# One product of the first layer normalisation, on VectorE instead of GpSimd

## The chip, the cores and the metric

The kernel runs on one core of a Trainium2 chip. The time is device microseconds of one execution, the median of several runs: 138.59 us before the change (three runs, 138.46 to 138.66). Beside the times there is one profiled execution with its trace. The engines are called as the profile calls them: PE (TensorE, matmuls) with PEld (its weight loads), DVE (VectorE), ACT (ScalarE), POOL (GpSimd) and SP (SyncE, which here only issues transfers).

## What is computed

One decoding step of a transformer layer for a batch of four tokens: layer normalisation, attention over a window of a cache, and a gated feed-forward part, each added to its input.

```
def _layernorm(x, axis=-1, eps=1e-5):
    m = jnp.mean(x, axis=axis, keepdims=True)
    v = jnp.var(x, axis=axis, keepdims=True)
    return (x - m) / jnp.sqrt(v + eps)

def _A_ref(x, k_cache, v_cache, wq, wo):        # 32 heads of 128, 4 key/value heads
    W = min(4096, max(256, Sk // 4))            # 2048 of 8192 positions
    q = (x @ wq).reshape(B, Sq, Hq, Dh).transpose(0, 2, 1, 3)
    k = jnp.repeat(k_cache[:, :, Sk - W:, :], rep, axis=1)
    v = jnp.repeat(v_cache[:, :, Sk - W:, :], rep, axis=1)
    p = _softmax(jnp.einsum("bhqd,bhkd->bhqk", q, k) * (Dh ** -0.5))
    o = jnp.einsum("bhqk,bhkd->bhqd", p, v)
    return o.transpose(0, 2, 1, 3).reshape(B, Sq, Hq * Dh) @ wo

def _B_ref(x, w1, w3, w2):                      # 1024 -> 3584 -> 1024
    return (_silu(x @ w1) * (x @ w3)) @ w2

h  = x + _A_ref(_layernorm(x), ...)
h2 = h + _B_ref(_layernorm(h), ...)
```

All inputs and the output are bf16. With four tokens every weight and every cached key and value is used for very little arithmetic: 55.6 MB are read for a result of 8 KB.

## The kernel before

All large inputs pass through one buffer in SBUF, `ring`, of five units of 32 KB in each of the 128 partitions. SyncE issues their loads in one fixed order (`load`, L127): `wq` in two pieces (slice 0 of eight, then slices 1 to 7), four loads of keys, four of values, `wo`, `w1`, `w3`, and `w2` in six pieces. A load whose place in the ring is still in use waits on SyncE's queue, and with it the loads behind it: the last two loads of values take the place of `wq`, so they wait for the query projection (L249); `w1` waits for the second attention output (L397); `w3` for the output projection (L484). ScalarE issues the small load of `x` (L139) and shares the output stores with SyncE.

The order of all work is written out by hand (`manual_schedule`), one program for each engine; an instruction that needs another engine's result waits on a semaphore, and a second wait at one place takes a semaphore instruction of its own. The stages are:

1. GpSimd builds identities, masks and constants (L147 to L201).
2. `x` is transposed on VectorE (L234) and normalised (`layernorm_T`, below), which gives `n_T`: the normalised input, transposed, as 8 slices of 128 partitions by 32 columns, of which 4 columns hold the tokens and the rest is zero.
3. The query projection: 64 matmuls (L249), eight for each of the eight slices of `wq`, with `n_T` as the stationary operand. The result is copied to SBUF (L259), transposed (L262), and spread into `Qm` (L269), which GpSimd has filled with zeros (L266).
4. Keys are transposed on TensorE (L283) and copied back by VectorE and ScalarE in turn (L285, L287), scores computed (L306), softmax (L318 to L378), attention outputs (L397), GpSimd sums (L414, L415).
5. The output projection (L484), the residual, and the second normalisation by the same `layernorm_T`.
6. The gate and up projections (L510), the gating, and the down projection (L560, L608), whose second part follows the landing of the last pieces of `w2`. VectorE and ScalarE write the result (L641 to L646) and four small stores take it out.

`layernorm_T` works on 8 slices by 4 tokens, 32 columns, in each of 128 partitions. ScalarE writes the input and its squares to `both` (L206, L207); one matmul with a matrix of 1/1024 sums over the partitions (L209); VectorE adds the eight slices (L211), which gives mean and mean square; GpSimd forms the variance (L215, L216); ScalarE takes the root (L217); VectorE the reciprocal, `rstd` (L220). Meanwhile GpSimd fills `n_T` with zeros (L222) and subtracts the mean, which gives `hc` (L224). The last step is the product of `hc` and `rstd` into `n_T` (L227). Behind it on GpSimd stand the fills of `Qm` and `oP` (L266, L268). The buffers of a normalisation (`both`, `mean`, `rstd`, `hc`) are the same ones both times; `n_T` has one for each.

Of the kernel before, what the change touches and what calls it, by code (L numbers as in the profile page):

```python
# [21 lines left out]
def kernel(  # L22
# [20 lines left out]
    nc = tc.nc  # L43

    B, _, D = A_x.shape
# [11 lines left out]
    S = R // B  # L57
# [142 lines left out]
        out=gather[:, :, :B], in_=ident[:].rearrange("p (c b s) -> p c b s", c=C, b=B)[:, :, :, 0]  # L200
    )  # L201

    def layernorm_T(h_T, tag):

        both = act.tile([P, 2, KC, B], FP32, tag="ln_both")
        nc.scalar.copy(out=both[:, 0], in_=h_T)  # L206
        nc.scalar.activation(out=both[:, 1], in_=h_T, func=ACT.Square)  # L207
        sums_ps = ps.tile([P, 2, KC, B], FP32, tag="scB")
        nc.tensor.matmul(sums_ps[:], lhsT=mean_f[:], rhs=both[:], start=True, stop=True)  # L209
        mean = act.tile([P, 2, B], FP32, tag="ln_mean")  # L210
        nc.vector.tensor_reduce(  # L211
            out=mean[:], in_=sums_ps[:].rearrange("p t k b -> p t b k"), axis=AX.X, op=ALU.add
        )
        rstd = act.tile([P, 1, B], FP32, tag="ln_rstd")
        nc.gpsimd.tensor_tensor(out=rstd[:, 0], in0=mean[:, 0], in1=mean[:, 0], op=ALU.mult)  # L215
        nc.gpsimd.tensor_tensor(out=rstd[:, 0], in0=mean[:, 1], in1=rstd[:, 0], op=ALU.subtract)  # L216
        nc.scalar.activation(  # L217
            out=rstd[:, 0], in_=rstd[:, 0], func=ACT.Sqrt, bias=eps_t[:], scale=1.0
        )
        nc.vector.reciprocal(out=rstd[:, 0], in_=rstd[:, 0])  # L220
        n_T = act.tile([P, KC, R], BF16, tag=tag + "_nT")
        nc.gpsimd.memset(n_T[:], 0.0)  # L222
        hc = act.tile([P, KC, B], FP32, tag="ln_hc")
        nc.gpsimd.tensor_tensor(  # L224
            out=hc[:], in0=both[:, 0], in1=mean[:, 0:1, :].to_broadcast([P, KC, B]), op=ALU.subtract
        )
        nc.gpsimd.tensor_tensor(  # L227
            out=n_T[:, :, :B], in0=hc[:], in1=rstd[:].to_broadcast([P, KC, B]), op=ALU.mult
        )
        return n_T  # L230

    def transpose_quads(dst, src, n):

        nc.vector.transpose(  # L234
            out=dst.rearrange("p j r -> p (j r)"), in_=src.rearrange("p (q j) -> p j q", j=n)
        )

    x_T = act.tile([P, KC, R], BF16, tag="xT")
    transpose_quads(x_T[:], x_nat[:], KC)
    xn_T = layernorm_T(x_T[:, :, ::S], "ln1")  # L240


    q_ps = ps.tile([P, 2, REP // 2, Dh], FP32, tag="scA")
# [253 lines left out]
        nc.scalar.copy(out=h1[2 * R * k : 2 * R * k + 2 * R, :], in_=y_ps[:, k])  # L497
    h_T = act.tile([P, KC, R], FP32)
    transpose_quads(h_T[:], h1[:], KC)
    hn_T = layernorm_T(h_T[:, :, :B], "ln2")  # L500


    FJ = FC // 2
# [180 lines left out]
```

## Time and profile before

| what | value |
|---|---|
| median of three runs | 138.59 us |
| the profiled execution's own time | 138.48 us |
| its span, first to last instruction | 136.7 us |
| bytes read | 55.58 MB |
| mean granted clock of TensorE | 0.871 |
| transfer of `wo` lands (SyncE's wait for it) | 82.0 us |
| last wait for a transfer ends on TensorE | 132.88 us |

Times inside the trace are microseconds from the start of the span. In a line of the page such as `PE 80.7 (59%) x779` stand the busy time, its share of the span and the number of instructions. A line of a timeline has the start, the duration, engine, line, operation, the names written and read, and in brackets how long the engine had been idle before and what ended that. A line of the chain of waits has the start, the duration and what ran. A line of the table of stretches has the stretch and its length, then the busy time of PE, PEld, DVE, ACT and POOL with the number of instructions, then TensorE's granted clock, the mean busy share of the sixteen DMA engines, and GB/s. The packet records, which the trace holds behind these views, give start, duration and size of each packet that a DMA engine moved; a load ends with one packet of four bytes on each engine that took part.

### The profile page before, as it was taken

How to read it: one execution, taken by the hardware profiler on the slowest of the kernel's cores; microseconds unless marked ns; L12 is line 12 of the kernel's file. 1: busy time of each engine (PE TensorE's matmuls, PEld its weight loads, DVE VectorE, ACT ScalarE, POOL GpSimd, SP SyncE). 2: the span in 40 equal slices, each digit the busy share in tenths (PEclk: the TensorE clock that was granted, in tenths of full speed). 3: DMA queues.
4: the chain of work that ended last, by engine and by line, in shares of the span. 5: the costliest groups of instructions: out<-in, count | busy, mean ns of one | idle time of the engine just before them, and what ended most of it. 6: DMA issues, size and time to landing. Idle time of an engine off the chain costs nothing.

```text
span 136.7 us, 1804 instructions
## 1 busy us (share of the span) xinstructions
PE 80.7 (59%) x779; PEld 43.5 (32%) x779; DVE 48.6 (36%) x45; ACT 29.9 (22%) x35; POOL 17.7 (13%) x50
## 2 busy tenths in 40 slices
PE   0000044959999985129992993995198000999770
PEld 0000022449966941023332340541043000444440
DVE  0000110007625463899299922001100297062022
ACT  3000140027959495013000000002501700000100
POOL 7600061000000000000084633000300000001000
PEclk9999999999999999855698699999856855569998
DMA  4999697999999999998978979969899798999960
GB/s 168 525 420 538 269 537 307 436 417 446 417 422 441 412 432 422 417 590 360 556 326 384 537 326 475 520 285 537 352 453 508 302 520 364 397 414 423 403 235 2
DMA packets 2782, 55.69 MB, mean 407 GB/s; under 512 B 312, under 2 KB 600, under 8 KB 728
## 3 DMA queue, kind: packets, MB, share of 16 engines
q1 hardware_dynamic: 2740, 55.58, 95.3%
q8 instruction: 6, 0.10, 0.3%
q10 hardware_dynamic: 36, 0.01, 0.0%
HBM read 55.58 MB, written 0.01 MB: 407 GB/s over the span
## 4 chain that ended last, share of the span: by engine, by line
DMA 56%; PE 30%; DVE 6%; ACT 3%; SPq 1%; issue 1%; DVEq 0%
DMA ring<-in_B_w_dram 40%; DMA ring<-in_A_wq_dram 16%; PE kt_ps L283 9%; PE sc_ps L306 5%; PE o_ps L397 5%; PE gate L510 4%; PE q_ps L249 4%; DVE P L360 2%; DVE PT L382 2%; SPq L128 1%; ACT ring L287 1%; PE small L397 1%; DVE ring L285 1%; DVE rmax L318 1%; ACT q_sb L259 1%
## 5 line engine op out<-in xcount | busy, mean ns | idle before, releaser
L287 ACT COPY ring<-kt_ps 128x2048 bf16<-128x2048 bf16 x8 | 14.6, 1866 | 7.1 <-PE kt_ps L283 7.1
L283 PE MATMUL kt_ps<-ident,ring 128*128 128x128 bf16 x256 | 15.0, 219 | 0.6 <-DVE Qm L269 0.5
L283 PEld LDWEIGHTS <-ring 128*128 128x128 bf16 x256 | 14.4, 98 | 2.6 <-issue 1.7
L414 POOL TENSOR_TENSOR o<-od 128x256 f32<-128x256 f32 x4 | 6.8, 1696 | 55.5 <-DVE od L405 55.5
L285 DVE COPY ring<-kt_ps 128x2048 bf16<-128x2048 bf16 x8 | 9.8, 1225 | 9.3 <-PE kt_ps L283 9.3
L510 PE MATMUL up<-ring,n_T 128*32 128x448 bf16 x64 | 6.0, 568 | 10.9 <-DMA ring<-in_B_w_dram 10.9
L209 PE MATMUL sums_ps<-both,mean_f 128*128 128x64 f32 x4 | 1.1, 366 | 19.0 <-ACT both L207 19.0
L397 PE MATMUL o_ps<-ring,PT 128*128 128x512 bf16 x32 | 11.5, 541 | 0.0
L510 PEld LDWEIGHTS <-n_T 128*32 128x32 bf16 x128 | 5.1, 143 | 20.3 <-DMA ring<-in_B_w_dram 11.5
L397 PEld LDWEIGHTS <-PT 128*128 128x128 bf16 x64 | 7.6, 121 | 10.3 <-issue 5.7
L532 DVE RECIPROCAL eg<-eg 128x896 f32<-128x896 f32 x1 | 5.8, 5753 | 10.9 <-ACT eg L531 10.9
L360 DVE TENSOR_TENSOR P<-p,gmask 128x2048 bf16<-128x2048 bf16 x4 | 9.1, 2278 | 0.8 <-ACT p L347 0.8
L382 DVE STREAM_TRANSPOSE PT<-P 128x2048 bf16<-128x2048 bf16 x4 | 9.2, 2306 | 0.1
L249 PE MATMUL q_ps<-ring,n_T 128*32 128x512 bf16 x64 | 6.2, 556 | 3.6 <-DMA ring<-in_A_wq_dram 1.8
L306 PE MATMUL sc_ps<-ring,Qm 128*32 128x512 bf16 x64 | 7.6, 605 | 0.4 <-DVE ring L285 0.4
L510 PE MATMUL gate<-ring,n_T 128*32 128x448 bf16 x64 | 5.9, 558 | 3.0 <-DMA ring<-in_B_w_dram 3.0
L397 PE MATMUL small<-ring,PT 128*128 128x512 bf16 x32 | 7.2, 379 | 0.0
L484 PE MATMUL y_ps<-ring,oP 128*32 128x512 bf16 x64 | 7.1, 379 | 0.1
L209 PEld LDWEIGHTS sums_ps<-both,mean_f 128*128 128x128 f32 x4 | 0.8, 249 | 19.4 <-issue 17.1
L234 DVE STREAM_TRANSPOSE x_T<-x_nat 128x256 bf16<-128x256 bf16 x1 | 0.6, 626 | 15.9 <-DMA x_nat<-in_A_x_dram 15.9
L560 PE MATMUL early_ps<-ring,hg_T 128*32 128x512 bf16 x42 | 5.0, 379 | 1.1 <-DMA ring<-in_B_w_dram 1.1
L464 ACT CAST oP<-on_ps 128x128 bf16<-128x128 f32 x1 | 0.3, 266 | 22.6 <-PE on_ps L457 22.6
(94 smaller groups left out, 68.9 us busy)
## 6 DMA issues: line engine op xcount, KB each, us to landing
ring<-in_B_w_dram SPq DMA_DIRECT2D x2, 7168.0 KB
ring<-in_A_k_cache_dram SPq DMA_DIRECT2D x4, 2048.0 KB, 25.6
ring<-in_A_v_cache_dram SPq DMA_DIRECT2D x4, 2048.0 KB, 42.8
ring<-in_A_wq_dram SPq DMA_DIRECT2D x1, 7168.0 KB, 21.2
ring<-in_B_w_dram SPq DMA_DIRECT2D x1, 3328.0 KB
ring<-in_B_w_dram SPq DMA_DIRECT2D x1, 2048.0 KB, 23.3
ring<-in_A_wq_dram SPq DMA_DIRECT2D x1, 1024.0 KB, 4.5
ring<-in_B_w_dram SPq DMA_DIRECT2D x1, 1024.0 KB
```

The lines of the kernel that those rows point to most:

```text
L249: nc.tensor.matmul(q_ps[R * c : R * c + R, hf], lhsT=xn_T[:, kc, :], rhs=wq_s[:, kc, o : o + HALF * Dh], start=(kc == 0), stop=(kc == KC - 1),
L283: nc.tensor.transpose(out=kt_ps[:, jj], in_=blocks[:, jj, :], identity=ident[:])
L285: nc.vector.tensor_copy(out=blocks, in_=kt_ps[:])
L287: nc.scalar.copy(out=blocks, in_=kt_ps[:])
L306: nc.tensor.matmul(sc_ps[b // 2][R * q : R * q + R, b % 2], lhsT=Qm[:, b, g * R : (g + 1) * R], rhs=kT[:, b, g, q], start=(g == 0), stop=( ...
L360: nc.vector.tensor_tensor(out=P4[:], in0=stage.pop(("p1", b))[:].rearrange("p (x o) -> p x o", o=1).to_broadcast([P, JR * L5, Hkv]), in1=g ...
L382: nc.vector.transpose(out=PT[:].rearrange("p j h -> p (j h)"), in_=stage.pop(("P4", b))[:].rearrange("p x g -> p (x g)"),)
L397: nc.tensor.matmul(o_ps, lhsT=PT[:, i * JM : (i + 1) * JM, :].rearrange("p j h -> p (j h)"), rhs=v_s[b][:, i * JM : (i + 1) * JM, :], star ...
L414: nc.gpsimd.tensor_tensor(out=o2[:], in0=od[:, :2], in1=od[:, 2:], op=ALU.add)
L484: nc.tensor.matmul(y_ps[R * i : R * i + R], lhsT=oP[:, t, :], rhs=row[:, i], start=False, stop=(t == T - 1), tile_position=(0, R * i), ski ...
L510: nc.tensor.matmul(out_ps[hf][R * c : R * c + R, :], lhsT=hn_T[:, kc, :], rhs=cols[:, kc, c, hf], start=(kc == 0), stop=(kc == KC - 1), ti ...
L532: nc.vector.reciprocal(out=eg[:], in_=eg[:])
```

## The change

`layernorm_T` takes the engine of its last product as an argument. The first normalisation passes VectorE, the second GpSimd, as before. All other instructions keep their engines and their order.

```
-    def layernorm_T(h_T, tag):
+    def layernorm_T(h_T, tag, eng):
...
-        nc.gpsimd.tensor_tensor(
+        eng.tensor_tensor(
             out=n_T[:, :, :B], in0=hc[:], in1=rstd[:].to_broadcast([P, KC, B]), op=ALU.mult
         )
         return n_T
...
-    xn_T = layernorm_T(x_T[:, :, ::S], "ln1")
+    xn_T = layernorm_T(x_T[:, :, ::S], "ln1", nc.vector)
...
-    hn_T = layernorm_T(h_T[:, :, :B], "ln2")
+    hn_T = layernorm_T(h_T[:, :, :B], "ln2", nc.gpsimd)
```

VectorE's program has two instructions more than before: the product and a wait.

## The prediction

> **What bounds the kernel now.** I read the page first for how busy each engine is, then a table of stretches, then the chain of waits, and last the order of instructions around the first normalisation. The first question is which resource has no idle time.
>
> ```profile
> PE 80.7 (59%) x779; PEld 43.5 (32%) x779; DVE 48.6 (36%) x45; ACT 29.9 (22%) x35; POOL 17.7 (13%) x50
> DMA packets 2782, 55.69 MB, mean 407 GB/s; under 512 B 312, under 2 KB 600, under 8 KB 728
> q8 instruction: 6, 0.10, 0.3%
> HBM read 55.58 MB, written 0.01 MB: 407 GB/s over the span
> ```
>
> No compute engine is busy for more than 59% of the span, while 55.58 MB of weights and cache are read. The stretches show where the DMA engines pause (the last two columns are their busy share and the rate):
>
> ```profile
> 2.00:22.00 20.00, 1.70 (x10) 0.79 (x11) 1.03 (x3) 3.27 (x5) 6.00 (x26) 1.00 1.01 429
> 22.00:42.00 20.00, 17.82 (x259) 13.02 (x259) 6.42 (x6) 9.15 (x6) 0.00 (x0) 1.00 1.01 429
> 62.00:82.00 20.00, 17.34 (x62) 7.18 (x61) 14.84 (x11) 0.78 (x2) 7.43 (x6) 0.78 0.98 423
> 102.00:122.00 20.00, 9.05 (x104) 3.82 (x96) 8.48 (x4) 3.15 (x3) 0.00 (x0) 0.59 0.95 409
> 132.00:137.00 5.00, 1.22 (x31) 0.66 (x18) 0.71 (x2) 0.26 (x1) 0.00 (x0) 0.86 0.08 26
> ```
>
> They don't pause: from 2 us to 132 us the share is about 1 (a packet counts in the stretch where it starts, hence 0.95 and 1.01). So the time is a start of about 2 us, a stream of 130 us, and a tail. The chain of waits seems to say something else for the middle:
>
> ```profile
> 22.44 5.17 PE q_ps L249 x56
> ...
> 68.07 1.74 PE small L397 x8
> 69.81 0.02 issue
> 69.83 29.46 DMA ring<-in_B_w_dram
> ...
> 132.84 0.04 issue
> 132.88 0.36 PE y_ps L608 x6
> ```
>
> From 22.44 to 69.81 us it runs through TensorE, since the w1 load (L448) is issued only once L397 has freed its ring space. But the DMA engines still had the wo load to move then: SyncE's next load waits 12.2 us more for wo, until about 82.0. The w1 load moves 7168 KB (7.34 MB), which at 429 GB/s takes 17.1 us; it ends at 99.28, and 82.0 + 17.1 = 99.1. So it flowed right behind wo, and its issue had some 12 us to spare. TensorE's early work is on the printed chain, yet it doesn't set the end.
>
> Now the place of the change:
>
> ```profile
> 18.79 0.24 POOL L224 TENSOR_TENSOR hc<-both,mean 128x32 f32<-128x32 f32 x1
> 18.95 0.18 DVE L220 RECIPROCAL rstd<-rstd 128x4 f32<-128x4 f32 x1 [0.93 <-ACT rstd L217]
> 19.27 0.24 POOL L227 TENSOR_TENSOR n_T<-hc,rstd 128x32 bf16<-128x32 f32 x1 [0.25 <-DVE rstd L220]
> 19.45 0.63 POOL L266 MEMSET Qm<- 128x640 bf16 x1
> 19.57 1.04 PE L249 MATMUL q_ps<-ring,n_T 128*32 128x512 bf16 x8 [1.81 <-POOL n_T L227]
> 22.44 5.15 PE L249 MATMUL q_ps<-ring,n_T 128*32 128x512 bf16 x56 [1.83 <-DMA ring<-in_A_wq_dram]
> ```
>
> The product ends at 19.51. Eight matmuls follow, on the first slice of wq, which is there; then TensorE stands for 1.83 us until the other seven slices have landed.
>
> **The change part by part.** *Removed from GpSimd:* one product of 0.24 us and the semaphore instruction before it (17 ns). *Added to VectorE:* a wait and a product; these are its two instructions.
>
> When can the product start? The reciprocal ends at 18.95 + 0.18 = 19.13. Now the hand-over to GpSimd takes 19.27 - 19.13 = 0.14 us. A VectorE instruction that waits for VectorE's own last result is in the trace: the reciprocal of L532 ends at 108.64 + 5.75 = 114.39 and L533 starts at 114.50, 0.11 us. So the start is about 19.24. The other input, hc, ends at 19.03 and is there.
>
> How long is it? No VectorE product of 32 columns is in the trace. From below, the reciprocal of 128x4 took 178 ns; from above, the copy of 128x128 took 292 ns. Between the products of 448 (625 ns) and 896 columns (1092 ns) a column costs 467/448 = 1.04 ns, and 625 - 416 x 1.04 = 192 ns for 32; the reduction of 64 columns took 224. I take 0.21 us. The product then ends at 19.45, 0.06 us sooner than now. By the ends, it starts at 19.20 to 19.27 and lasts 0.18 to 0.29: 19.38 to 19.56, so from 0.13 sooner to 0.05 later.
>
> *TensorE's wait.* Its first weight load of L249 waits for GpSimd alone, as both the zeros of n_T (L222) and the product come from there. Afterwards they come from two engines. Where TensorE already waits for two at one place, a semaphore instruction of its own stands there (51 ns at L320; GpSimd's at L227 took 17 ns). I add one such: 0.02 us, 0.05 at most. The zeros are written by 18.83, so it holds nothing up. Queued behind it is TensorE's whole program, so its cover matters. The first eight matmuls end at about 20.57 (20.71 at worst) instead of 20.61, and the next needs wq at 22.44. The shift is swallowed by that idle time: 0.00 us. If that cover were gone, the same 0.13 sooner to 0.10 later would reach q and the scores, and the 12 us of the w1 load would swallow it there.
>
> *Queued behind, elsewhere.* On VectorE it is the copy to Qm (L269), at 29.43, ten microseconds on. On GpSimd the zeros of Qm and oP move up from 19.45 to about 19.1; L269, at 29.43, is the first to need them. In the second normalisation the product stays on GpSimd, and its buffers were last read by VectorE some 78 us before. No DMA is moved past anything.
>
> *Do the two engines hinder each other?* GpSimd's sum at L414 took about 2.7 us beside VectorE's products and 0.72 us without, so they can. Here it would stretch the zeros of Qm, say fourfold to 2.5 us: done by 22.6 with those of oP, still 6.8 us early. Were VectorE the one to stand instead, for the 0.63 us of one fill, the product would end at 20.1 and the eight matmuls at 21.2, before 22.44. Nothing in both cases.
>
> The sum: 138.48 (the profiled execution: 136.7 span and 1.8 around it) + 0.00. That execution lies 0.11 below the median of the three runs, so against the median I forecast 138.6.
>
> **The rivals.** *First, a clock that dips in the tail (slower).* TensorE's granted clock is 0.59 between 102 and 122 us and 1.00 from 122 to 132. If a half-speed stretch falls on the last landing, the six matmuls between it and VectorE's result (0.36 us) take 0.72: 138.59 + 0.36 = 138.95. It decides from the point where the half-speed stretch that now ends at 122 lasts to 133. For it: the stretches begin and end at multiples of 3.41 us from each other (57.13, 67.37, 74.20, 77.61), and the change moves TensorE's first burst by a few hundredths. Against: three runs lie within 0.2 us, and TensorE's 2.4 us of idle time between 124 and 133 soaks up a short dip. [...]
>
> *Second, an instruction block that meets a loaded DMA engine (slower).* The page lists six instruction packets; in the packet records each is 16 KB and takes 1.03 to 1.10 us, at 34.0, 40.7, 50.0, 82.4, 105.6 and 130.8 us, every one in step with TensorE's program. What they do can be read from the sixteen completions of each load: before the first they lie within 0.55 us; after it one engine is 1.3 us late, then two, three, four and five, the same lateness each, so each block hit another engine. The one 128 KB load in 16 partitions makes four more engines late by 1.8 us. They finish last, at 132.72; those that a block delayed finish just before. One instruction more in TensorE's program, or another start of it, could put a block on one of those four: the end moves by about 1.65 (late completions at 128.35 to 128.48 against the others at about 126.8), 140.2. For it: the margin between good and bad is one engine. Against: six blocks remain six, since the seventh edge would lie some 250 instructions on and TensorE has some 40 left; VectorE's program has about 70 instructions and no block of its own in the span. [...]
>
> *Third, the end of the stream evens out (faster).* The engines end their last loads between 132.1 and 132.72. If the blocks fell so that all ended at the mean, about 132.4, the tail would start 0.3 sooner: 138.3. For it: the same sensitivity. Against: the four engines with the small load stay late whatever the blocks do.
>
> *Fourth,* the change doesn't come to pass as said, for instance the product waits again behind GpSimd's fills (0.63 + 0.95 us): n_T at 21.0, the eight matmuls done by 22.1, still hidden; 138.6.
>
> **How the numbers follow.** A difference of 0.2%, 0.28 us, is about what a measurement of this kernel can tell from no change. The forecast, all hidden, gets 0.58, the fourth case 0.04: same 0.62. The clock gets 0.11, the block 0.08, and 0.05 goes to what I don't see on that side: slower 0.24. The evened end gets 0.10, and 0.04 for the unseen: faster 0.14. The range reaches below to the evened end with a tenth for the spread of the runs, 138.2, and above to the clock's 138.95 and as much as the runs' spread of 0.2 again, 139.2; it leaves out the block and part of the unseen. The likeliest case alone is 138.4 to 138.8.
>
> **What would show it.** Right: VectorE's product of 128x32 near 0.2 us, n_T's first use at 19.4 to 19.6, TensorE idle before 22.4 for 1.8 to 2.0 us, the last landing near 132.8, DMA share near 1 throughout. Wrong: wq landing at another time; seven instruction packets, or one followed by completions 3 us late; a granted clock of 0.5 around 133; or any new wait of SyncE's queue that ends after the DMA engines have run dry.

## The result, and the profile after

The changed kernel takes 139.89 us (median of five runs, 139.81 to 140.02) against 138.58 us before: a ratio of 1.0098, 95% interval 1.0083 to 1.0113. It is 1.3 us slower. The forecast was 138.6, no change, and the range ended at 139.2.

The page of the profile after, with the span, the busy times and the DMA queues:

```profile
span 137.6 us, 1802 instructions
PE 79.3 (58%) x777; PEld 42.9 (31%) x779; DVE 48.7 (35%) x46; ACT 29.9 (22%) x35; POOL 17.5 (13%) x49
DMA packets 2783, 55.70 MB, mean 405 GB/s; under 512 B 312, under 2 KB 600, under 8 KB 728
q8 instruction: 6, 0.10, 0.3%
q14 instruction: 1, 0.01, 0.0%
```

Two things are to be seen. The span grew by 0.9 us only, so some 0.5 us of the loss lies around it. And there is one packet more than before, on a queue that the page of before doesn't list: an instruction packet.

First the place of the change, in the timeline after:

```profile
19.09 0.24 POOL L224 TENSOR_TENSOR hc<-both,mean 128x32 f32<-128x32 f32 x1
19.25 0.18 DVE L220 RECIPROCAL rstd<-rstd 128x4 f32<-128x4 f32 x1 [0.93 <-ACT rstd L217]
19.27 0.63 POOL L266 MEMSET Qm<- 128x640 bf16 x1
19.53 0.19 DVE L227 TENSOR_TENSOR n_T<-hc,rstd 128x32 bf16<-128x32 f32 x1
19.77 1.04 PE L249 MATMUL q_ps<-ring,n_T 128*32 128x512 bf16 x8 [1.72 <-DVE n_T L227]
22.49 5.29 PE L249 MATMUL q_ps<-ring,n_T 128*32 128x512 bf16 x56 [1.67 <-DMA ring<-in_A_wq_dram]
```

The product takes 0.19 us on VectorE and ends 0.29 us after the reciprocal, where it was 0.38 before. (All of the stage lies 0.3 us later, since x landed 0.3 us later in this execution.) TensorE then waits 1.67 us for wq, as it did. Nothing was lost here. The stretches after show the stream as full as before, and the chain of waits ends it at nearly the same time:

```profile
2.00:22.00 20.00, 1.70 (x10) 0.78 (x11) 1.22 (x4) 3.27 (x5) 5.78 (x25) 1.00 1.00 428
102.00:122.00 20.00, 9.21 (x108) 4.07 (x100) 9.47 (x6) 3.15 (x3) 0.00 (x0) 0.66 0.95 408
132.00:137.00 5.00, 1.39 (x40) 0.84 (x29) 0.81 (x3) 0.26 (x1) 0.00 (x0) 0.90 0.08 26
```

```profile
133.04 0.04 issue
133.08 0.36 PE y_ps L608 x6
```

The loss is in the last four microseconds, behind the last landing. SyncE waits there for the output stores (engine and line, what it waited for, us in total, times, longest). Before:

```profile
SPq L679 <- DMA out_dram<-res: 1.0, 2, 0.7
```

and after:

```profile
SPq L679 <- DMA out_dram<-res: 2.0, 2, 1.8
```

Behind the stores comes the closing barrier of the program (listed under L679). An engine enters it with a drain, which here ends 0.05 us behind the engine's last computing instruction (VectorE before: 134.05 and 134.01). Its instructions on VectorE, by the view of that line (duration in ns, shortest, median and longest, then the first and last start), before:

```profile
L679 DVEq EVENT_SEMAPHORE  x2: 21/21/21, 135.8 to 136.6; - x2
L679 DVEq DRAIN  x2: 143/322/500, 133.6 to 136.3; - x2
```

and after:

```profile
L679 DVEq EVENT_SEMAPHORE  x2: 21/21/21, 137.1 to 137.6; - x2
L679 DVEq DRAIN  x2: 19/134/248, 134.0 to 137.2; - x2
```

Before, VectorE was released in the barrier at 135.80 and started its second drain at 136.32, half a microsecond later; after, it follows within 0.11 (137.09 to 137.21). Its first drain shows the reverse: before, it started at 133.55, beside the last result instruction (L646, 133.58); after, at 134.01, 0.23 us behind it. So the barrier before held a stall of 0.4 us that is gone, and yet the end is later. The records of the trace put the pieces together. For each kernel that was run: the start of VectorE's first result instruction (L642, right behind the last landing; where lines were added it has a later number), the last store's completion after that, from there to the end of the span, what the execution took outside the span, its time, and when 8 KB instruction packets moved (from the start of the span on).

```
                     L642   store   barrier  around   time    8 KB packets
                     starts done    to end   span
before              133.26   2.17    1.25     1.79   138.48   136.99 137.18
after               133.47   3.26    0.90     2.26   139.89   134.66 138.63
two fills only      133.63   3.39    1.24     1.79   140.05   135.14 138.76
length undone       133.77   2.17    1.27     2.03   139.24   137.76 137.92
GpSimd's length     133.63   3.44    1.27     1.79   140.13   135.18 138.82
one fill            133.54   2.18    1.24     1.89   138.85   135.68 137.46
both edges early    134.18   2.17    0.91     1.79   139.05   118.20 127.22
one and five        133.75   2.17    0.92     1.79   138.62   128.43 135.71
five on GpSimd      134.62   2.17    1.26     1.83   139.88   127.50 138.37
two and five        134.39   3.26    0.91     1.83   140.39   127.93 135.59
product, old length 133.61   2.18    1.27     1.79   138.85   137.35 137.54
beside the stores   133.43   2.17    0.90     1.87   138.38   135.68 136.39
```

After against before: 0.21 at L642, 1.09 at the stores, -0.35 in the barrier, 0.47 around the span; together 1.4, the difference of the two profiled executions.

The stores' part shows in the packet records after. Each of the four stores moves four packets of 512 bytes, on four DMA engines. The instruction packet runs from 134.66 to 135.25; one packet of each store starts at 135.25, 135.28, 135.31 and 135.34, right behind it, while the other twelve had ended by 135.10. Three of the four completions of the last store come at 135.61 to 135.64 and the fourth at 136.72. Before, all four came at 135.30 to 135.43.

### The profile page after: what moved, and what is told of

It is laid out like the page before. It is cut to its first block, busy times and chain, and to the rows that moved or that the text cites. A ratio compares the mean times of both kernels' runs of the same rounds, so it can differ in the third digit from the quotient of the medians.

```text
span 137.6 us, 1802 instructions
## 1 busy us (share of the span) xinstructions
PE 79.3 (58%) x777; PEld 42.9 (31%) x779; DVE 48.7 (35%) x46; ACT 29.9 (22%) x35; POOL 17.5 (13%) x49
## 4 chain that ended last, share of the span: by engine, by line
DMA 56%; PE 30%; DVE 6%; ACT 3%; SPq 1%; issue 1%; DVEq 0%
DMA ring<-in_B_w_dram 40%; DMA ring<-in_A_wq_dram 15%; PE kt_ps L283 9%; PE sc_ps L306 5%; PE o_ps L397 4%; PE gate L510 4%; PE q_ps L249 4%; DVE P L360 2%; DVE PT L382 2%; ACT ring L287 1%; SPq L128 1%; PE small L397 1%; DVE ring L285 1%; DVE rmax L318 1%; ACT q_sb L259 1%
## 5 line engine op out<-in xcount | busy, mean ns | idle before, releaser
L510 PE MATMUL up<-ring,n_T 128*32 128x448 bf16 x64 | 4.5, 452 | 10.8 <-DMA ring<-in_B_w_dram 10.8
```

Source lines behind the costliest of these rows:

```text
L510: nc.tensor.matmul(out_ps[hf][R * c : R * c + R, :], lhsT=hn_T[:, kc, :], rhs=cols[:, kc, c, hf], start=(kc == 0), stop=(kc == KC - 1), ti ...
```

## The experiments

The theory that came out of this, called the length theory below, is my reading of the packet records: each instruction packet (8 KB at 136.99 and 137.18 before, at 134.66 and 138.63 after) is taken for a block of one engine's program; VectorE's program, two instructions longer, meets a block's edge two instructions earlier, ahead of its first drain instead of ahead of its second, and the packet that goes with the edge then moves together with the stores (0.59 us from 134.66) and holds up one of their DMA engines. The rival, the product theory: it is the product on VectorE itself, or what it shifts behind the normalisation. Medians and ratios below are against the kernel before on the same chip, whose median was 138.80 for the first four, 138.61 for the next four and 138.73 for the last two.

The fills that make a program longer are all of this kind, ahead of the normalisation, where both engines have nothing to do:

```
+    pad = const.tile([1, 64], FP32)
+    for i in range(2):
+        nc.vector.memset(pad[:, i : i + 1], 0.0)
...
     def layernorm_T(h_T, tag):
```

**Two fills only.** The edit above on the kernel before; the product stays on GpSimd.

> The kernel before, product on GpSimd, with two fills of one number each put early into VectorE's program. Length theory (VectorE's program, two instructions longer, reaches the edge of an 8 KB instruction block before its last drain, and the fetch of the next block holds up one of the DMA engines that carry the output stores): an 8 KB instruction packet near 134.6 us, the last store's completion 1.1 to 1.3 us later than before, 139.4 if GpSimd's program of the old length costs nothing, up to 139.9 if it stands at its own edge in the last barrier. Product theory (what costs is the product on VectorE, in the first normalisation): 138.6, no packet at 134.6.

139.96 us, ratio 1.0083 (1.0068 to 1.0098). Nearly the whole loss, 1.16 of 1.31 us, is there without the change. The page and SyncE's waits of this kernel:

```profile
span 138.3 us, 1804 instructions
...
q14 instruction: 1, 0.01, 0.0%
...
SPq L683 <- DMA out_dram<-res: 2.2, 2, 1.9
```

The packet is there, at 135.14, and SyncE's longest wait for the stores is 1.9 us. The barrier is 1.24 long although VectorE's stall is gone from it; the time around the span is 1.79. So this kernel loses in the barrier what the changed one loses outside.

**The length undone.** The changed kernel, with a small copy that runs twice moved from VectorE to ScalarE, and two fills on GpSimd.

```
-        nc.vector.tensor_copy(out=bias[:], in_=nm_ps)
+        nc.scalar.copy(out=bias[:], in_=nm_ps)
...
+    for i in range(2):
+        nc.gpsimd.memset(pad[:, 32 + i : 33 + i], 0.0)
```

> The changed kernel, product on VectorE, but VectorE's program two instructions shorter elsewhere (the two small copies of the bias, L341, on ScalarE) and two fills added on GpSimd, so both programs have the length of before. Length theory: 138.6, no instruction packet of 8 KB before 136.9, VectorE's stall of 0.45 us back in the last barrier. Product theory: 139.9 still.

139.63 us, 1.0053 (1.0037 to 1.0068), with nine runs from 139.00 to 140.01: neither expectation. The tail of the profiled execution (139.24) is as the length theory expected: stores done after 2.17, packets at 137.76 and later, VectorE's second drain 0.5 us late. But the time is not that of before, and the copy on ScalarE changed more than the length: TensorE and ScalarE got an instruction more each, L642 starts 0.5 us later, and the runs spread over 1 us. Its tail speaks for the length theory; its time decides nothing. The ninth experiment does it more cleanly.

**GpSimd's length back.** The changed kernel with the two fills on GpSimd alone.

> The changed kernel with two fills added on GpSimd, so that only VectorE's program is longer than before. The span grew by 0.94 us and the time around it by 0.5. If the 0.5 is GpSimd's program, two instructions shorter, which meets its own block edge after the span: the time around the span is back to 1.8 us, the 8 KB packet after the span comes earlier, and the stall moves into the last barrier (span 138.0) or vanishes (span 137.6): 139.9 or 139.4. If the 0.5 has to do with VectorE alone: around the span 2.3, 139.9.

139.91 us, 1.0077 (1.0060 to 1.0094). The time around the span is back at 1.79, and the barrier is at 1.27 instead of 0.90. So the 0.47 us around the span were GpSimd's: by the length theory its program, two instructions shorter, met its own edge behind the last instruction of the span. With the old length it meets it in the barrier, where VectorE's stall had covered it before. The time is as good as that of the changed kernel, 1.1 us above the kernel before: what left the space around the span came back in the barrier.

**One fill.** The kernel before with one fill on VectorE.

> The kernel before with one fill put early into VectorE's program. Length theory: the edge lies one instruction later than in the changed kernel, behind the drain, where VectorE waits for the stores anyway; the fetch comes near 135.4, after the stores' packets: no delay of the stores, 138.1 to 138.6 (138.1 if only VectorE's stall was on the path of the last barrier, 138.6 if GpSimd stands there as long). Without the length theory one instruction more should cost half of what two cost: about 139.2.

138.82 us, 0.9999 (0.9990 to 1.0008). One instruction costs nothing, two cost 1.2 us. Of the length theory's two cases it is the one in which GpSimd stands in the barrier as long. The lines of this kernel, of SyncE's waits, the queues and the barrier:

```profile
SPq L683 <- DMA out_dram<-res: 1.0, 2, 0.7
...
q14 instruction: 1, 0.01, 0.0%
...
L683 DVEq DRAIN  x2: 24/265/506, 133.8 to 136.2; - x2
```

The packet is in the span as in the changed kernel, but at 135.68, when the stores' packets had ended (135.23): they are not late. VectorE's second drain comes at 136.21, 0.12 after its release at 136.09. Now it is GpSimd that stands: 0.38 us between its last drain's end (136.39) and its next instruction (136.77), against 0.04 after. That is why the barrier is no shorter.

**Both edges early.** The changed kernel with four fills more on VectorE and seven on GpSimd.

> The changed kernel, product on VectorE, with four fills more early in VectorE's program (six instructions more than before) and seven on GpSimd (five more than before). Length theory: VectorE meets its edge while it waits for the last matmuls and GpSimd while it waits for the stores, so the stall of some 0.45 us that one of the two showed in the last barrier of each kernel so far is gone, VectorE's packet comes near 133, ahead of the stores, and GpSimd's near 125 to 126: 0.4 us below the kernel before on the same chip, the product on VectorE notwithstanding. Product theory: 1.1 to 1.3 us above it.

139.03 us, 1.0038 (1.0023 to 1.0054), 0.4 above, which neither theory has. The product is on VectorE and about two thirds of its supposed cost (1.1 to 1.3) is absent, but the gain that the length theory forecast isn't there either. Both stalls are gone (0.91), but both packets moved in the stream of weights, at 118.2 and 127.2, VectorE's far sooner than expected, and there they cost too. Of the four completions of the small load that lands after the first packet, one comes at 125.07, 0.9 us behind the next; in the loads after the second packet another is 0.5 us late as well, and L642 starts at 134.18.

**One and five fills.** The kernel before, one fill on VectorE, five on GpSimd.

> The kernel before with one fill more on VectorE and five on GpSimd. Length theory: with one alone the stall of 0.4 us stood on GpSimd instead of VectorE; with five there too nobody stands in the last barrier, VectorE's packet comes behind the stores: 0.4 us below the kernel before. If the stall on GpSimd isn't what held the barrier: no change.

138.71 us, 1.0018 (1.0003 to 1.0033). The barrier is 0.92: with one fill alone it was GpSimd that stood there. What this saves, GpSimd's packet at 128.4 takes back in the stream: the last completion of the last load comes at 133.66, 0.38 us behind the next. In the four kernels with a packet in the stream that gap is 0.38 to 0.70 us, in the other eight at most 0.30. In size this is less sure, since L642 starts as late as here (133.75) in a kernel without such a packet too (133.77 with the length undone).

**Five fills on GpSimd alone.**

> The kernel before with five fills more on GpSimd alone. Length theory: VectorE still stands 0.45 us at its edge in the last barrier, so no change, within 0.1 us of the kernel before. If GpSimd's edge alone held the barrier: 0.4 us below.

139.46 us, 1.0062 (1.0043 to 1.0080), which neither expectation has. VectorE's stall is in the barrier as expected (1.26). The rest is ahead of the stores: GpSimd's packet at 127.50 makes the next piece of w2 late in one of its sixteen completions (129.84, the others by 129.12), and the chain of waits of this execution then runs through matmuls at a lower clock (the second line is of the table of stretches, its granted clock third from the end):

```profile
129.88 3.02 PE early_ps L564 x16
```

```profile
132.00:135.00 3.00, 2.65 (x45) 1.54 (x40) 1.18 (x4) 0.26 (x1) 0.00 (x0) 0.68 0.16 55
```

Before, the same sixteen took 1.90 us. How much of the median is the packet and how much the clock, one profile can't say.

**Two and five fills.** The kernel before, two on VectorE, five on GpSimd.

> The kernel before with two fills more on VectorE and five on GpSimd. Length theory: VectorE's packet meets the stores as in the changed kernel, which costs 1.1 us, and no stall is left in the last barrier, which saves 0.4: 0.6 to 0.8 us above the kernel before. If the delay of the stores and the stalls aren't separate sums: 1.1 to 1.3 above.

139.61 us, 1.0069 (1.0055 to 1.0084), 1.0 above; between the two expectations. GpSimd's packet moved in the stream here too (127.93, and the last completion of the last load is 0.61 us behind the next). The profiled execution, at 140.39 the slowest of the five, also shows a lower clock (0.65 between 132 and 135), so what each of the two added is not told apart. Stores and barrier add up as separate pieces: the stores 3.26 as in the changed kernel, the barrier 0.91 as with both edges away.

**The product on VectorE at the old length.** The changed kernel without the reciprocal, and one fill on GpSimd.

```
-        nc.vector.reciprocal(out=rstd[:, 0], in_=rstd[:, 0])
...
+    for i in range(1):
+        nc.gpsimd.memset(pad[:, 32 + i : 33 + i], 0.0)
```

> The changed kernel, product on VectorE, without the reciprocal in either normalisation (L220 left out, so the product is with the root itself): VectorE's program is then as long as before, and one fill brings GpSimd's to its length of before. TensorE's and ScalarE's programs are untouched. Length theory: the time of the kernel before within 0.2 us, no instruction packet before the stores are done, VectorE's stall back in the last barrier. Product theory: 1.1 to 1.3 us above.

138.81 us, 1.0000 (0.9991 to 1.0009). With the product on VectorE and the lengths of before, the time is that of before, and so is the tail: the queues list no packet of that kind in the span, SyncE's wait and VectorE's late drain are back.

```profile
q1 hardware_dynamic: 2740, 55.58, 95.2%
q8 instruction: 6, 0.10, 0.3%
q10 hardware_dynamic: 36, 0.01, 0.0%
...
SPq L682 <- DMA out_dram<-res: 1.0, 2, 0.7
...
L682 DVEq DRAIN  x2: 144/320/496, 133.9 to 136.7; - x2
```

**The edges beside the stores.** The kernel before with one fill on VectorE, three on GpSimd, and a last GpSimd instruction that waits for the first store, so that GpSimd meets its edge while the other stores run.

```
                 out=out_flat[:, c * DQ : (c + 1) * DQ], in_=res[R * c : R * c + B, :]
             )
+            if c == 0:
+                nc.gpsimd.memset(res[:B, :1], 0.0)
```

> The kernel before with one fill on VectorE, which puts VectorE's edge behind its drain, three on GpSimd, and one more on GpSimd at the end that waits for the first output store, so that GpSimd meets its edge while the last stores are under way, behind the stream and ahead of the barrier. Length theory: no block is fetched in the stream, none before the stores, and nobody stands in the last barrier: 0.4 us below the kernel before. If a block of GpSimd's still meets the stores or is asked for early, in the stream: as before or 0.3 to 1 us above, and its packet will show where.

138.47 us, 0.9977 (0.9969 to 0.9986): faster than both kernels, by 0.3 us against before. The packets are at 135.68 and 136.39, behind the stores' packets, the stores are done after 2.17, the barrier takes 0.90.

```profile
span 136.5 us, 1810 instructions
...
q14 instruction: 2, 0.02, 0.0%
...
SPq L687 <- DMA out_dram<-res: 1.0, 2, 0.7
```

## Why the prediction was wrong

*What was right.* The product takes 0.19 us (0.21 forecast), ends 0.09 sooner after the reciprocal (0.06 forecast), and is swallowed by the wait for wq (1.67 us); the fills on GpSimd move up and nobody notices; the stream stays full; TensorE's chain through the middle doesn't set the end. The ninth experiment shows the cost of the product itself: none, within 0.1%. One detail was wrong without consequence: TensorE got no semaphore instruction more (12 before and after).

*The step that failed* is in the second rival: "VectorE's program has about 70 instructions and no block of its own in the span". The mechanism of that rival, a block that meets a loaded DMA engine, is by the length theory the one that struck, but I tied it to TensorE's program and to the weights, priced it at 1.65 us there and gave it 0.08. I read "in the span" as "far from it". The records of before had two 8 KB instruction packets at 136.99 and 137.18, 0.3 and 0.5 us behind the span's end, and a drain of VectorE's that stood 0.4 us in the closing barrier: by the length theory VectorE was at an edge already, two instructions from its first drain (one fill has the packet at 135.68, two have it at 135.14), with the stores right before it. So the sum put two instructions more on VectorE at 0.00 once their run time was hidden; two empty ones alone measured 1.16 us, 1.09 of the changed kernel's loss is in the stores, and with the product on VectorE but the lengths of before nothing is lost. The prediction's own sign came, seven instruction packets in the span, on VectorE's side instead of TensorE's.

*The second failure* is the sum's "1.8 around it", taken as fixed. It held the other half of the edit: GpSimd's program became two instructions shorter, by the length theory its edge moved behind the span (a packet at 138.63), and the time around it became 2.26. Two fills put it back to 1.79. In the whole time this mattered little, since the barrier then took 1.27 instead of 0.90: 1.11 us above the kernel before with GpSimd's length back, 1.31 without.

*The other rivals.* The clock did dip in the tail, most in two profiles with a packet in the stream (0.68 and 0.65 between 132 and 135), but not in that of the changed kernel (1.00 from 122 to 135). The end of the stream didn't even out: the last completion comes at 133.36 against 133.17 before.

*The packets by size.* In the records before, the six packets in the span, taken for TensorE's, have 16 KB each. Between one and the next, 190 to 289 recorded instructions of TensorE start (matmuls, weight loads, semaphores), 240 on average, where the prediction has some 250; behind the sixth 83 start, 40 of them matmuls, where it has some 40 in all. Six packets remained six: they are in the records after too, with 86 behind the last. The packets taken for VectorE's and GpSimd's have 8 KB. What came with their edges at the end of this kernel was 0.35 us in the barrier, 0.47 us behind the span and 1.09 us in the stores.

*What stays open.* The packet ends at 135.25 and the held-up store packets by 135.37, but their completions come another 0.9 to 1.4 us later, where those of the other twelve come within about 0.5 of their packets; the records show nothing in between, so that the packet's own 0.6 us is only part of the 1.09. That they share a DMA engine is concluded from the order of the packets, since the records name no engine; which instruction packet is VectorE's and which GpSimd's is concluded from when they move with the fills. Nor is the stall a wait for the packet that follows it: before, VectorE went on at 136.32 and the first packet moved at 136.99; with one fill, GpSimd went on at 136.77 and the packet moved at 137.46. What the engine waits for at an edge, the records don't show. The 0.2 us by which L642 starts later after the change is the lateness of one completion of the last load (133.36; the others had ended by 133.17, as before) and isn't explained; among the kernels with no early packet it varies from 133.26 to 133.77.

## What to carry to other kernels

Two instructions more on VectorE, at a place where their own time is hidden, cost 1.2 to 1.3 us, as two empty fills (139.96 against 138.80) and as the product with its wait (139.89 against 138.58); two fewer on GpSimd went with 0.47 us more around the span. By the length theory the edit moved every later instruction of its engine against the edges of that engine's blocks, in the program that lost instructions as in the one that gained them. Look in the packet records for instruction packets near the start of the last stores and just behind the span, and for an engine that is late in the closing barrier. Where such a packet or such a stall is found, test the edit against one that only adds or removes as many empty instructions before crediting or blaming what it computes.

## What the runs showed that was not expected

- The time is no steady function of the length: with 0, 1 and 2 fills on VectorE it was 138.8, 138.8 and 140.0 us.
- A packet of 8 KB that meets the stores makes them 1.1 to 1.3 us later in every one of the four kernels where the two coincide (3.26 to 3.44 against 2.17 to 2.18 in the other eight).
- VectorE and GpSimd stood 0.3 to 0.4 us at an edge in the closing barrier, each covering the other's stall: taking VectorE's away alone gained nothing (138.82 against 138.80). Taking both away gained 0.3 us in the one kernel of four where no packet met the stream or the stores.
- With six instructions more, the packet taken for VectorE's came at 118.2 us, 16 us ahead of L642 (134.18); why it came so early the records don't show. This was seen once and not tried further.
